# VectorE's own landing signal for K tiles, and a later place for w1, in a two-layer decode kernel

## The chip, the cores and the metric

The kernel runs on one core of one Trainium2 chip. A core has five engines with instruction queues of their own: PE (TensorE, matrix products), DVE (VectorE), ACT (ScalarE), POOL (GpSimd) and SP (SyncE, which here only issues transfers). They tell each other of finished work by semaphores. Sixteen DMA engines move data between the chip's memory (HBM) and the core's on-chip memory (SBUF, 128 partitions). The metric is the device time of one execution in microseconds (us), as the median of several runs.

## What is computed

Two identical rounds (called layers) of attention over a cache and a small mixer MLP, for one new token and a batch of two:

```python
x = A_x                                              # [2, 1, 576]
for _ in range(2):
    x = x + A(layernorm(x))
    x = x + B(layernorm(x))

def A(x):                                            # 32 heads of 128, 16384 cached positions
    q = (x @ wq).reshape(B, 1, 32, 128).transpose(0, 2, 1, 3)
    scores = einsum("bhqd,bhkd->bhqk", q, k_cache) * 128 ** -0.5
    o = einsum("bhqk,bhkd->bhqd", softmax(scores), v_cache)
    return o.transpose(0, 2, 1, 3).reshape(B, 1, 4096) @ wo

def B(x):
    h = gelu(layernorm(x) @ w1)
    hs = shifted(h) @ w2                             # shifts along a sequence of length 1
    x1 = x + hs
    return x1 + gelu(layernorm(x1) @ w3) @ w4
```

All inputs are bf16. K and V hold 2 x 32 x 16384 x 128 values each, 268 MB, and both layers read both of them. The shifts move every value of `h` out of a sequence of length one, so `hs` is the product of zeros with w2; the kernel computes `h` nevertheless, for both layers at once, at its very end.

## The kernel before

**Units and steps.** A unit is one head of one batch row; there are U = 64. Its K is one tile and its V another: 128 partitions x 32,768 bytes, 4.19 MB. A step of `attention` (L773 on) works on the K tile of one unit and the V tile of the unit before. Layer 0 takes the units in order; layer 1 starts with the last three (62, 63, 61), of which tiles are still on chip, and goes on with 0 to 60.

**What a step does.** The K tile has 128 blocks of 128 positions. PE and VectorE share them: for half of the blocks PE transposes eight at a time (`transposes`, L895), ScalarE copies them out of PSUM (`evacuate`, L906) and PE multiplies them with q (`scores`, L917); for the other half VectorE multiplies by a broadcast q and sums (`dots`, L943 and L947), four pairs of instructions in a step. The loop over `c` (0 to 7) writes the order of all engines down: scores run two chunks behind the transposes, so the last two chunks of a step are scored in the next step, at c = 0 and c = 1. VectorE's first pair of a step is at c = 0, the others at c = 2, 4 and 6; after the second pair come the maxima of the step before (`softmax_max`, L954 to L958), GpSimd's reduction over partitions (L960), and, on ScalarE, the exponentials (`softmax_exp`). PE's product with V (`pv`, L1001) is in four parts at c = 4 to 7. At c = 6 VectorE prepares the next unit's q (`q_broadcast`, L857 and L860), PE spreads it over the partitions (L864), and ScalarE copies it to `qb` (L867).

**Hardware loops and signals.** The steps 2 to 61 of layer 0 and 4 to 63 of layer 1 are "turning": three steps make one turn of a loop on PE, ACT and DVE, 120 steps in all. Inside a loop an engine can only wait on semaphores that belong to it alone (`_turn`: "a wait that no loop can hold"). The landing of a transfer has a semaphore without an owner. So GpSimd, which is not looped, waits for each landing and passes it on: `relay` (an increment, emitted at L201), called by `landed` at the start of a step for K and before `pv` for V. The relay's semaphore belongs to PE. VectorE learns of a landed K tile from PE: the score chunk that PE runs at c = 0 (after its first transposes of the new tile) writes the name `"go"`, and VectorE's first multiply of the step reads it.

**Slots and the plan.** On-chip memory for streamed data has six slots of the size of a tile (T bytes each). `plan_all` writes down, in order, every transfer of the kernel and its place. `Store.pump` issues the entries of this list strictly in order: if the head of the list needs cells that are still owned, everything behind it waits. A tile is released when its last reader is emitted; for a K tile in a turning step that is the last score of the step (c = 7). All transfers go through SP's queue (L100), which waits there for the readers of the old contents. In layer 1 the slots go round as (3, 0, 2, 5, 4, 1), so the end of the list of tiles is: (k,59) to slot 4, (v,58) to 1, (k,60) to 3, (v,59) to 0, (v,60) in two halves to 2. Then follow the weights: wo in three row pieces (slots 4, 4, 5), w3 in five pieces (slots 5, 5, 1, 1, 1), w4 in six (slots 1, 3, 3, 3, 3, 3). w1 of layer 1 (three DMAs of 576, 63 and 9 KB) lies in slot 4 behind wo's second piece; it is read by `h_projection` (L1049) after the output has been sent off. Its entry stands before the last two tiles, (v,59) and (v,60):

```python
        for i, (t, u) in enumerate(tiles):
            if i == len(tiles) - 2:
                self.plan_small("w1", 1, self.w1, 4 * T + 22 * row, (0, 56, 64))
            plan = self.plan_halves if i in (2, 4, len(tiles) - 1) else self.plan_tile
            plan(self.K if t == "k" else self.V, t, u, place[i])
```

**After the loop.** The last step (s = U) finishes the last unit; then `normalize`, wo, layer norms, w3 (L652, L657), gelu, w4 (L723), the transposes of the result and the transfer out follow, each bound to the one before.

Of the kernel before, what the change touches and what calls it, by code (L numbers as in the profile page):

```python
# [16 lines left out]
class Op:  # L17
# [4 lines left out]
    def __init__(self, eng, fn, sig=None, col=None):  # L22
        self.eng, self.fn, self.sig, self.col = eng, fn, sig, col
        self.deps, self.waits = [], []
        self.needed = self.relay = False
        self.val = self.sem = self.know = self.own = None

    @property
    def stream(self):
        return self.sem if self.sem is not None else "relay" if self.relay else self.eng  # L30


class Graph:
# [44 lines left out]
    def op(self, eng, fn, reads=(), writes=(), sig=None, col=None):  # L78
        return self._add(Op(eng, fn, sig, col), reads, writes)

    def relay(self, reads, writes):

        o = Op("gpsimd", None)
        o.relay = True
        return self._add(o, reads, writes)

    def dma(self, sem, starts, reads=(), writes=()):
# [45 lines left out]
    def emit(self):  # L133
        nc = self.nc
        self._waits()
        inside = {e: set() for e in self.LOOPED}
        for e in self.LOOPED:
            for first, (n, turns) in self.loops[e].items():
                inside[e].update(range(first, first + n * turns))
        users = {}  # L140
        for o in self.all:
            for d in o.waits:
                d.needed = True
                if o.eng in self.LOOPED and o.pos in inside[o.eng] and d.sem is None:
                    users.setdefault(id(d), set()).add(o.eng)
        for e in self.LOOPED:
            ops = self.ops[e]
            for first, (n, turns) in self.loops[e].items():
                for i in range(first, first + n):
                    same = ops[i:i + n * turns:n]  # L150
                    assert all(o.sig is not None and o.sig == same[0].sig for o in same), [o.sig for o in same]
                    some = any(o.needed for o in same)
                    who = set().union(*(users.get(id(o), ()) for o in same))
                    for o in same:
                        o.needed = some
                        if who:
                            users[id(o)] = who
                    if same[0].col is not None:
                        step = same[1].col - same[0].col
                        assert all(o.col == same[0].col + t * step for t, o in enumerate(same)), [o.col for o in same]  # L160
        done = {e: nc.alloc_semaphore(f"done_{e}") for e in self.ENGS if e != "sync"}
        own = {}
        count = {}
        for e in self.ENGS:
            for o in self.ops[e]:
                if o.sem is not None:
                    continue
                who = users.get(id(o), set())
                assert len(who) <= 1, (e, o.sig, who)
                o.own = "tensor" if o.relay else next(iter(who), None)  # L170
                o.needed = o.needed or o.relay
                if o.needed:
                    k = (o.stream, o.own)
                    count[k] = count.get(k, 0) + 1
                    o.val = count[k]
                    if o.own and k not in own:
                        own[k] = nc.alloc_semaphore(f"{o.stream}_{o.own}")
        for o in self.all:
            for d in o.waits:
                assert d.own in (None, o.eng), (o.eng, o.sig, d.eng, d.sig)  # L180

        def handle(k):
            s, who = k
            return self.dma_sems[s] if s in self.dma_sems else own[k] if who else done[s]

        def wait(eng, need, seen):
            for k, v in need.items():
                if v > 0 and seen.get(k, 0) < v:
                    eng.wait_ge(handle(k), v)
                    seen[k] = v  # L190

        def needs(o):
            need = {}
            for d in o.waits:
                k = (d.stream, d.own)
                need[k] = max(need.get(k, 0), d.val)
            return need

        def emit_op(eng, o, col=None):
            if o.relay:  # L200
                eng.sem_inc(own["relay", o.own], 1)  # L201
                return
            ins = o.fn(eng) if o.col is None else o.fn(eng, o.col if col is None else col)
            if o.sem is None and o.needed:
                ins.then_inc(handle((o.stream, o.own)), 1)

        def runner(e):
            def run(eng):
                seen, taken = {}, {}
                ops = self.ops[e]  # L210
                i = 0
                while i < len(ops):
                    if i in self.loops.get(e, ()):
                        n, turns = self.loops[e][i]
                        taken = self._turn(eng, ops, i, n, turns, taken, wait, needs, emit_op, handle)
                        seen = {k: v for k, v in seen.items() if not k[1]}
                        i += n * turns
                        continue
                    o = ops[i]
                    wait(eng, {k: v - taken.get(k, 0) for k, v in needs(o).items()}, seen)  # L220
                    emit_op(eng, o)
                    i += 1
            return run

        with nc.Block() as block:
            for e, sect in (("sync", block.sync), ("scalar", block.scalar), ("tensor", block.tensor),
                            ("vector", block.vector), ("gpsimd", block.gpsimd)):
                if self.ops[e]:
                    sect(runner(e))
# [93 lines left out]
class KB:  # L323
# [131 lines left out]
    def plan_all(self):  # L455

        T, U, n = self.TILE, self.U, self.KT - 1
# [4 lines left out]
        tiles = self.tile_order(0)  # L462
# [18 lines left out]
        tiles = self.tile_order(1)  # L481
        place = [0, 3] + [(3, 0, 2, 5, 4, 1)[i % 6] for i in range(2, len(tiles))]
        for i, (t, u) in enumerate(tiles):
            if i == len(tiles) - 2:
                self.plan_small("w1", 1, self.w1, 4 * T + 22 * row, (0, 56, 64))
            plan = self.plan_halves if i in (2, 4, len(tiles) - 1) else self.plan_tile
            plan(self.K if t == "k" else self.V, t, u, place[i])
        self.cuts["wo", 1] = [(0, 11, 4 * T), (11, 22, 4 * T + 11 * row), (22, 32, 5 * T)]
# [2 lines left out]
        self.cuts["w4", 1] = [(0, 8, w4_at)] + \  # L491
                             [(a, b, 3 * T + (a - 8) * row) for a, b in ((8, 16), (16, 24), (24, 30), (30, 34), (34, 36))]
        self.plan_rows("wo", 1, self.wo, self.cuts["wo", 1])
        self.plan_cols("w3", 1, self.w3, [at, at + w3r, T, T + w3r, T + 2 * w3r])
        self.plan_rows("w4", 1, self.w4, self.cuts["w4", 1])

# [265 lines left out]
    def attention(self, l):  # L762
# [4 lines left out]
        pend = []  # L767
# [9 lines left out]
        for s in range(U + 1):  # L777
# [5 lines left out]
            if l and s == U:  # L783
                self.home()
            if s < U and not self.kept(l, s):
                self.landed(l, "k", o[s])
            prompt, after = self.prompt(l, s), self.prompt(l, s - 1)
            n = self.pb(l, s) // self.CH
            for c in range(2 * n):
# [6 lines left out]
                    pend.append((s, u, c, self.chunk))  # L796
                    self.chunk += 1
                while pend and (len(pend) > LEAD or s == U):
                    self.scores(*pend.pop(0), go=turning and c == 0, of=(l, o[s]) if end else None)
                if s < U:  # L800
                    if c == 0 and prompt and s >= 1:
                        self.q_broadcast(o[s + 1], s + 1)
                    if c % n in (0, 2):
                        self.dots(l, s, u, h, c % n // 2, go=turning and c == 0)
                    if c == 2 * n - 2 and not prompt and s + 1 < max(U, leave + 1):
                        self.q_broadcast(o[s + 1] if s + 1 < U else u + 1, s + 1)
                if after:
# [35 lines left out]
        for t, k in ((self.o_acc, "o_acc"), (self.l, "l")):  # L843
            self.dv(lambda e, t=t: e.tensor_copy(out=t[:, at:at + 1], in_=t[:, 0:1]), reads=[k], writes=[k])

    def landed(self, l, t, u, last=False):

        if (t, u) in self.store.where:
            names = [(t, u)]
        else:  # L850
            names = [(t, u, h) for h in range(2)]
        for some in ([[nm] for nm in names] if last else [names]):
            self.g.relay([k for nm in some for k in self.store.keys(nm)], [("landed", nm) for nm in some])

    def q_broadcast(self, u, s):
        i = s % self.NS
# [50 lines left out]
                                        in_=self.tps[t][:, :].rearrange("p (i c) -> p i c", i=self.CH), func=ACT.Copy),  # L907
                 reads=[("tps", t)], writes=[("kt", k)], sig=("evac", c, t, k))

    def scores(self, s, u, c, at, go=False, of=None):  # L910

        k = at % self.NKT
        sp = s % self.NS
# [1 line left out]
        def f(pe):  # L915
# [1 line left out]
                ins = pe.matmul(self.sps[sp][:, c * self.CH + j:c * self.CH + j + 1], lhsT=self.kt[k][:, j, :],  # L917
                                rhs=self.q_col[:, sp:sp + 1], start=True, stop=True, skip_group_check=True)
            return ins
        reads, writes = [("q_col", sp), ("kt", k)], [("sps", sp)]  # L920
        if go:
            writes = writes + ["go"]
        last = []
        if of:
            for h in range(2):
                nm, _, keys = self.tile(of[0], "k", of[1], h * self.BP, self.BP)
                reads = reads + keys
                last.append(nm)
        self.pe(f, reads=reads, writes=writes, sig=("s", c, k, sp, go, of is not None))
        for nm in last:  # L930
            self.used(of[0], nm, self.CH)

    def dots(self, l, s, u, h, i, go=False):
        pb = self.pb(l, s)
        DB = (self.BP - pb) // 2
        r = s % self.NS
# [5 lines left out]
        c0 = (2 * h + i) * DB  # L942
        self.dv(lambda e: e.tensor_tensor(out=prod, in0=buf.rearrange("p (j d) -> p j d", d=128),  # L943
                                          in1=qbc, op=ALU.mult),
                reads=[("qb", r)] + keys + (["go"] if go else []), writes=["prod"], sig=("mult", r, c0, keys[0]))
        self.used(l, nm, DB)
        self.dv(lambda e: e.tensor_reduce(out=sd[:, c0:c0 + DB], in_=prod, axis=AX.X, op=ALU.add),  # L947
                reads=["prod"], writes=[("s_dve", r)], sig=("sum", r, c0))
# [159 lines left out]
```

## Time and profile before

| | |
|---|---|
| runs | 2597.4, 2594.4, 2595.95 us; median 2595.95 |
| profiled execution | 2597.14 us; span of its trace 2595.4 us |
| PE busy | 1598.9 us (62%) |
| VectorE busy | 1916.8 us (74%) |
| ScalarE busy | 1205.5 us (46%) |
| GpSimd busy | 51.5 us (2%) |
| SP's queue of transfers | 58798 packets, 1096.33 MB, 98.9% of 16 engines' span |
| VectorE L943 waiting for PE L917 | 529.9 us in 120 waits |
| chain that ended last | DVE 61%, PE 21%, issue 13%, DMA 3% |

How to read it. The page gives the busy time of each engine, and the span cut into 40 equal slices: a digit is the busy share of the slice in tenths, and the DMA row has the gigabytes per second under it. An answer by windows gives the same for any stretch: its bounds and length, the busy time and the number of instructions for PE, PEld (weight loads), DVE, ACT and POOL, the granted TensorE clock, the DMA share, GB/s. A row of the timeline is start, duration, engine, line and operation, result and operands; in brackets the idle time of the engine before it and who ended it. A row of waits is who waited, for whom, us in total, how often, and the longest. A row of issues ends with the median us from the issue of a transfer to its landing. "L943" is a line of the kernel.

### The profile page before, as it was taken

To read this page: it belongs to the slowest core of one execution; us is meant where nothing else is said; L and a number is where in the kernel's file an instruction comes from. 1 tells how busy PE (TensorE), PEld (TensorE's weight loads), DVE (VectorE), ACT (ScalarE), POOL (GpSimd) and SP (SyncE) were. 2 spreads that over 40 slices of the span, in tenths; PEclk is the share of its full clock that TensorE was granted. 3 is DMA by queue.
4 is the path that set the end of the run, shared out by engine and by line. 5 is a ranking of instruction groups with operands and counts; after the bars stand their busy time and mean duration, and the time that the engine had idled before them with its cause. 6 is when DMAs were issued, how large, how long until landed. Compare 5 with 4: busy or idle time off the path is not lost.

```text
span 2595.4 us, 74490 instructions
## 1 busy us (share of the span) xinstructions
PE 1598.9 (62%) x34309; PEld 1568.2 (60%) x34309; DVE 1916.8 (74%) x2048; ACT 1205.5 (46%) x1816; POOL 51.5 (2%) x149
## 2 busy tenths in 40 slices
PE   3656656656656656656666666666666666666665
PEld 3656656656656656656666665665665665665664
DVE  4777777777777777777568777777777777777773
ACT  3444544544544544544345444444444444444441
POOL 0000000000000000000000000000000000000000
PEclk8555655655555555555566555555555555555555
DMA  9999999999999999999999999999999999999959
GB/s 405 428 432 431 432 431 431 432 432 432 432 431 432 431 432 431 432 432 432 396 422 418 426 429 433 430 432 430 433 431 429 434 429 433 429 432 431 433 242 363
DMA packets 58851, 1097.09 MB, mean 423 GB/s; under 512 B 4778, under 2 KB 23342, under 8 KB 23854
## 3 DMA queue, kind: packets, MB, share of 16 engines
q1 hardware_dynamic: 58798, 1096.33, 98.9%
q8 instruction: 40, 0.66, 0.1%
q14 instruction: 13, 0.11, 0.0%
HBM read 1096.30 MB, written 0.00 MB: 422 GB/s over the span
## 4 chain that ended last, share of the span: by engine, by line
DVE 61%; PE 21%; issue 13%; DMA 3%; SPq 1%; DVEq 0%; ACT 0%; POOL 0%; POOLq 0%
DVE s_dve L947 33%; DVE prod L943 23%; PE tps L895 9%; PE mps L1001 8%; PE sps L917 2%; SPq L100 1%; PE sps L864 1%; DMA mem<-in_A_k_cache_dram 1%; DMA mem<-in_B_w_dram 1%; DVE diag L860 1%; DVE l L982 1%; DVE mx L956 1%; DVE q_col L857 1%; DVE mx L954 1%; DMA mem<-in_A_wo_dram 1%
## 5 line engine op out<-in xcount | busy, mean ns | idle before, releaser
L906 ACT ACTIVATE kt<-tps 128x1024 bf16<-128x1024 bf16 x1026 | 1037.2, 1024 | 710.1 <-PE tps L895 693.8
L947 DVE TENSOR_REDUCE s_dve<-prod 128x16 f32<-128x2048 bf16 x512 | 1168.3, 2282 | 17.6
L943 DVE TENSOR_TENSOR prod<-mem,qb 128x2048 bf16<-128x2048 bf16 x512 | 625.6, 1222 | 548.6 <-PE sps L917 529.9
L895 PE MATMUL tps<-ident,mem 128*128 128x128 bf16 x8208 | 998.2, 299 | 21.5 <-issue 13.1
L1001 PE MATMUL mps<-p,mem 128*128 128x1 bf16 x16384 | 515.0, 166 | 657.8 <-ACT p L973 639.0
L1001 PEld LDWEIGHTS mps<-p,mem 128*128 128x128 bf16 x16384 | 486.9, 104 | 669.0 <-ACT p L973 649.8
L895 PEld LDWEIGHTS tps<-ident,mem 128*128 128x128 bf16 x8208 | 762.0, 136 | 25.2 <-issue 16.6
L917 PEld LDWEIGHTS sps<-q_col,kt 128*128 128x128 bf16 x8208 | 411.3, 113 | 4.8 <-ACT kt L906 4.6
L917 PE MATMUL sps<-q_col,kt 128*128 128x1 bf16 x8208 | 400.3, 170 | 3.2 <-ACT kt L906 2.5
L968 ACT ACTIVATE mx<-mx 128x1 f32<-128x1 f32 x128 | 26.0, 203 | 386.0 <-POOL mx L960 386.0
L864 PE MATMUL sps<-diag,ones_bf 128*128 128x128 bf16 x129 | 37.1, 288 | 255.9 <-DVE diag L860 255.9
L864 PEld LDWEIGHTS sps<-diag,ones_bf 128*128 128x128 bf16 x129 | 13.5, 104 | 266.6 <-DVE diag L860 266.6
L867 ACT ACTIVATE qb<-sps 128x128 bf16<-128x128 f32 x129 | 35.8, 277 | 199.7 <-PE sps L864 199.7
L960 POOL PARTITION_ALL_REDUCE mx<-mx x128 | 49.3, 385 | 2487.8 <-DVE mx L958 2411.8
L970 ACT ACTIVATE p<-s_dve,mx 128x64 bf16<-128x64 f32 x128 | 44.5, 348 | 4.2
L973 ACT ACTIVATE p<-sps,mx 128x64 bf16<-128x64 f32 x128 | 37.6, 294 | 0.0
L956 DVE TENSOR_REDUCE mx<-sps 128x1 f32<-128x64 f32 x128 | 27.6, 215 | 11.7 <-PE sps L917 11.7
L723 PE MATMUL mps<-prod,mem 128*128 128x2 bf16 x680 | 20.7, 165 | 23.5 <-DMA mem<-in_B_w_dram 14.1
L723 PEld LDWEIGHTS mps<-prod,mem 128*128 128x128 bf16 x680 | 19.4, 104 | 25.0 <-DMA mem<-in_B_w_dram 12.2
L616 ACT ACTIVATE rstd<-rstd,eps 128x2 f32<-128x2 f32 x8 | 2.4, 295 | 65.8 <-DVE rstd L614 65.8
L860 DVE TENSOR_SCALAR diag<-ident,q_f 128x128 bf16<-128x128 bf16 x129 | 31.6, 245 | 0.3 <-PE sps L864 0.3
L703 DVE TENSOR_TENSOR x<-x,mps 128x8 f32<-128x8 f32 x4 | 0.7, 164 | 38.6 <-PE mps L723 38.6
(90 smaller groups left out, 245.3 us busy)
## 6 DMA issues: line engine op xcount, KB each, us to landing
mem<-in_A_v_cache_dram SPq DMA_DIRECT2D x124, 4096.0 KB, 32.1
mem<-in_A_k_cache_dram SPq DMA_DIRECT2D x122, 4096.0 KB, 31.3
mem<-in_B_w_dram SPq DMA_DIRECT2D x13, 1152.0 KB, 12.5
mem<-in_A_k_cache_dram SPq DMA_DIRECT2D x7, 2048.0 KB, 15.3
mem<-in_A_wq_dram SPq DMA_DIRECT2D x8, 1024.0 KB, 9.1
mem<-in_A_v_cache_dram SPq DMA_DIRECT2D x4, 2048.0 KB, 16.8
mem<-in_A_wo_dram SPq DMA_DIRECT2D x4, 1584.0 KB, 24.5
mem<-in_B_w_dram SPq DMA_DIRECT2D x6, 576.0 KB, 10.7
```

The costliest lines, as they stand in the source:

```text
L723: ins = pe.matmul(self.mps[:, t * B:(t + 1) * B], lhsT=buf[:, o:o + 128], rhs=rhs(k), start=(k == 0 and t == 0), stop=(k == last), skip_gr ...
L860: self.dv(lambda e, c: e.tensor_scalar(out=self.diag[:, :], in0=self.ident[:, :], scalar1=self.q_f[:, bass.ds(c, 1)], scalar2=None, op0=AL ...
L864: self.pe(lambda pe: pe.matmul(qps, lhsT=self.ones_bf[:, :], rhs=self.diag[:, :], start=True, stop=True, skip_group_check=True), reads=["o ...
L895: ins = pe.transpose(self.tps[t][:, j * 128:(j + 1) * 128], buf[:, j * 128:(j + 1) * 128], self.ident[:, :])
L906: self.act(lambda e: e.activation(out=self.kt[k][:, :, :], in_=self.tps[t][:, :].rearrange("p (i c) -> p i c", i=self.CH), func=ACT.Copy), ...
L917: ins = pe.matmul(self.sps[sp][:, c * self.CH + j:c * self.CH + j + 1], lhsT=self.kt[k][:, j, :], rhs=self.q_col[:, sp:sp + 1], start=True ...
L943: self.dv(lambda e: e.tensor_tensor(out=prod, in0=buf.rearrange("p (j d) -> p j d", d=128), in1=qbc, op=ALU.mult), reads=[("qb", r)] + key ...
L947: self.dv(lambda e: e.tensor_reduce(out=sd[:, c0:c0 + DB], in_=prod, axis=AX.X, op=ALU.add), reads=["prod"], writes=[("s_dve", r)], sig=(" ...
L956: self.dv(lambda e: e.tensor_reduce(out=mx[1], in_=self.sps[i][:, 0:n], axis=AX.X, op=ALU.max), reads=[("sps", i)], writes=[("mx1", i)], s ...
L960: self.pool(lambda e: e.partition_all_reduce(mx[3], mx[2], channels=128, reduce_op=ROP.max), reads=[("mx2", i)], writes=[("mx3", i)])
L970: self.act(lambda e: e.activation(out=p[:, n:self.NB], in_=self.s_dve[i][:, 0:self.NB - n], func=ACT.Exp, bias=mx[4], scale=self.scale, ac ...
L1001: ins = pe.matmul(self.mps[:, 448:449], lhsT=buf[:, j * 128:(j + 1) * 128], rhs=p[:, col:col + 1], start=(h == 0 and b == 0), stop=(h == 1 ...
```

## The change

GpSimd's `relay` now takes the engine that is to be told, and each such engine has a semaphore of its own (`landed_tensor`, `landed_vector`). In the turning steps `landed` sends two relays for a K tile, to PE and to VectorE, one after the other. VectorE's multiplies read the new name `("seen", tile)` where the first of them read `"go"`; the score chunk at c = 0 no longer writes `"go"`. In the plan of layer 1, w1's entry moves from before the last two tiles to between wo and w3; its place in memory stays. What is computed stays the same.

```diff
-    def relay(self, reads, writes):
+    def relay(self, to, reads, writes):
         o = Op("gpsimd", None)
-        o.relay = True
+        o.relay = f"landed_{to}"
+        o.own = to
         return self._add(o, reads, writes)
...
             if o.relay:
-                eng.sem_inc(own["relay", o.own], 1)
+                eng.sem_inc(own[o.stream, o.own], 1)
                 return
...
         for i, (t, u) in enumerate(tiles):
-            if i == len(tiles) - 2:
-                self.plan_small("w1", 1, self.w1, 4 * T + 22 * row, (0, 56, 64))
             plan = self.plan_halves if i in (2, 4, len(tiles) - 1) else self.plan_tile
...
         self.plan_rows("wo", 1, self.wo, self.cuts["wo", 1])
+        self.plan_small("w1", 1, self.w1, 4 * T + 22 * row, (0, 56, 64))
         self.plan_cols("w3", 1, self.w3, [at, at + w3r, T, T + w3r, T + 2 * w3r])
...
             if s < U and not self.kept(l, s):
-                self.landed(l, "k", o[s])
+                self.landed(l, "k", o[s], both=turning)
...
-                    self.scores(*pend.pop(0), go=turning and c == 0, of=(l, o[s]) if end else None)
+                    self.scores(*pend.pop(0), of=(l, o[s]) if end else None)
...
-                        self.dots(l, s, u, h, c % n // 2, go=turning and c == 0)
+                        self.dots(l, s, u, h, c % n // 2, told=turning)
...
         for some in ([[nm] for nm in names] if last else [names]):
-            self.g.relay([k for nm in some for k in self.store.keys(nm)], [("landed", nm) for nm in some])
+            keys = [k for nm in some for k in self.store.keys(nm)]
+            self.g.relay("tensor", keys, [("landed", nm) for nm in some])
+            if both:
+                self.g.relay("vector", keys, [("seen", nm) for nm in some])
...
-        reads, writes = [("q_col", sp), ("kt", k)], [("sps", sp)]
-        if go:
-            writes = writes + ["go"]
+        reads = [("q_col", sp), ("kt", k)]
...
-                reads=[("qb", r)] + keys + (["go"] if go else []), writes=["prod"], sig=("mult", r, c0, keys[0]))
+                reads=[("qb", r)] + keys + ([("seen", nm)] if told else []), writes=["prod"], sig=("mult", r, c0, keys[0]))
```

The rest of the diff renames what the two parts need.

## The prediction

> **What bounds the kernel now.** I read the page's slices and queue shares first, then the queue's own waits, then time-ordered rows around the odd slice, then the steady step.
>
> ```profile
> span 2595.4 us, 74490 instructions
> DMA  9999999999999999999999999999999999999959
> GB/s 405 428 432 431 432 431 431 432 432 432 432 431 432 431 432 431 432 432 432 396 422 418 426 429 433 430 432 430 433 431 429 434 429 433 429 432 431 433 242 363
> ```
>
> The page: the DMA engines are full from start to end, at 432 GB/s in a steady slice. A K or V tile is 128 x 32,768 B = 4.194 MB, so two of them (one step of the loop) take 8.389 / 0.432 = 19.42 us. One slice, the last but one, falls to 242 GB/s: of its 64.9 us, (432 - 242) / 432, some 28 us, are empty. The empty stretch, window by window (us, busy time of PE, PEld, DVE, ACT, POOL, clock, DMA share, GB/s):
>
> ```profile
> 2495.00:2500.00 5.00, 0.90 (x33) 0.90 (x34) 4.93 (x8) 0.94 (x5) 0.35 (x1) 0.60 0.99 426
> 2500.00:2505.00 5.00, 3.10 (x69) 3.02 (x66) 4.93 (x5) 2.05 (x2) 0.00 (x0) 0.50 0.00 0
> ...
> 2520.00:2525.00 5.00, 2.96 (x76) 2.88 (x74) 4.35 (x5) 2.24 (x3) 0.00 (x0) 0.50 0.00 0
> 2525.00:2530.00 5.00, 5.00 (x108) 5.00 (x106) 1.27 (x2) 2.63 (x4) 0.00 (x0) 0.50 0.42 125
> ```
>
> SP's longest wait from 2490 us on, and its issues in order of time:
>
> ```profile
> SPq L100 <- PE sps L917: 38.7, 1, 38.7
> ```
>
> ```profile
> 2487.64 0.33 SPq L100 DMA_DIRECT2D mem<-in_A_k_cache_dram  x1
> 2526.70 1.25 SPq L100 DMA_DIRECT2D mem<-in_B_w_dram  x3
> 2527.99 1.29 SPq L100 DMA_DIRECT2D mem<-in_A_v_cache_dram  x3
> 2529.33 24.84 SPq L100 DMA_DIRECT2D mem<-in_A_wo_dram  x3
> ```
>
> SP issued the last K tile, (k,60), at 2487.64 and then stood 38.7 us for a score of PE, because the next entry of the plan is w1. By the placement rule w1 lies in slot 4, which (k,59) holds until the last score of step 62. Behind it stood (v,59), whose slot 0 had been free since (v,56) was consumed in step 60, and (v,60), whose slot 2 came free a step before slot 4.
>
> Why is slot 4 so late? Landing times of K, in windows 100-200, 1100-1200, 1400-1500 and 2300-2400 us (last number: median us from issue to landing):
>
> ```profile
> mem<-in_A_k_cache_dram SPq DMA_DIRECT2D x5, 4096.0 KB, 33.4
> mem<-in_A_k_cache_dram SPq DMA_DIRECT2D x4, 4096.0 KB, 31.4
> mem<-in_A_k_cache_dram SPq DMA_DIRECT2D x5, 4096.0 KB, 15.0
> mem<-in_A_k_cache_dram SPq DMA_DIRECT2D x5, 4096.0 KB, 13.8
> ```
>
> They shrink slowly: compute is a hair slower than the transfers (19.33 us twice, 19.73 once in three issues, mean 19.46, against 19.42). In layer 1 a K tile lands some 14 us after issue and is used two steps, 39 us, after it: compute runs 25 us behind. (k,60) landed at 2487.64 + 13.9 = 2501.5 and its first multiply began at 2528.69. So the lag is compute's, and one step shows whose:
>
> ```profile
> 2465.79 0.25 DVE L860 TENSOR_SCALAR diag<-ident,q_f 128x128 bf16<-128x128 bf16 x1
> 2466.09 0.29 PE L864 MATMUL sps<-diag,ones_bf 128*128 128x128 bf16 x1 [2.04 <-DVE diag L860]
> ...
> 2466.42 0.28 ACT L867 ACTIVATE qb<-sps 128x128 bf16<-128x128 f32 x1 [1.50 <-PE sps L864]
> ...
> 2469.80 0.40 PE L917 MATMUL sps<-q_col,kt 128*128 128x1 bf16 x8
> ...
> 2470.30 1.23 DVE L943 TENSOR_TENSOR prod<-mem,qb 128x2048 bf16<-128x2048 bf16 x1 [4.27 <-PE sps L917]
> ```
>
> VectorE ends its step at 2466.04 and stands 4.27 us for the "go" score of PE, although its operands (the K tile, and qb at 2466.70) are there. Over the run that is 529.9 us in 120 waits, one for each loop step.
>
> **The semaphore edit.** It removes 120 waits on "go"; it adds 120 increments on GpSimd and, in the go's place, 120 waits of VectorE. Behind that wait stands everything VectorE does in a step (four multiplies and sums, the maxima, keep, diag), and GpSimd's all-reduce, ScalarE's exponentials and PE's PV matmuls wait for those. With the tile landed, the new wait ends at once and the multiply goes to qb: 2466.70 + 0.05 instead of 2470.30, 3.55 us earlier. The step's floor is then 19.33 - 3.55 = 15.78 us. Can PE keep that? Its first PV of a step comes 9.1 us after VectorE's first multiply (2450.97 to 2460.05); counted from 2466.75 that is 2475.8, and PE was through its transposes and scores at 2473.6. The maxima come 7.1 us after the multiply, at 2473.8, and the scores they need ended at 2471.3. Yes.
>
> The increment has no row of its own. The relay to PE at 2541.87 was followed by PE's matmul at 2542.01, so at most 0.14 us for both. GpSimd's sequencer holds the all-reduce behind it; GpSimd is busy 51.5 us of the run. Bounds over 120 steps: 0, and 120 x 0.14 = 17 us if nothing covered it. I take 0: the cover is 19.42 - 15.78 = 3.6 us of slack per step.
>
> But 3.55 us x 120 = 426 us isn't to be had: transfers at 19.42 take over as soon as the lag is eaten. In layer 1 25 us go at 3.6 us a step in seven steps; with 60 loop steps, 25 / 60 = 0.42 us a step would be enough. In the steady part the transfers were never idle, so the gain there is nothing. It is worth something where they starved at the entry of layer 1's loop:
>
> ```profile
> 1396.00:1400.00 4.00, 4.00 (x99) 4.00 (x100) 0.00 (x0) 1.42 (x3) 0.00 (x0) 0.50 0.83 291
> 1400.00:1404.00 4.00, 4.00 (x66) 4.00 (x62) 3.79 (x3) 3.87 (x4) 0.00 (x0) 0.54 0.90 385
> ```
>
> (432 - 291) / 432 x 4 + (432 - 385) / 432 x 4 = 1.7 us, bounds 0 and 3 (smaller dips near it). And it releases slot 4 about 20 us earlier, which the second edit needs.
>
> The DMA: Bandwidth & Descriptors page of the Trainium skill (Specifications) speaks against all this: it gives a core 358 GB/s from HBM. By that, two tiles would take an estimated 23.4 us, steps would be bound by transfers already, and the first edit would be worth nothing: about 2567. The slices say 432, and the trace decides.
>
> **w1 behind wo.** Moved: one wait and three DMAs of 576, 63 and 9 KB, issued in 1.25 us, on SP's queue past (v,59), the two halves of (v,60) and the three wo pieces. No other queue issues it. Its only reader is the projection at the very end (L1049, 2592.69). Before, (v,59) landed at 2527.99 + 13.9 = 2541.9. After, (k,60) is followed at once: 2501.5 + 9.71 = 2511.2, 30.7 us earlier. w1's 0.664 MB come back between wo and w3: 1.5 us at 432 GB/s, 1.8 at the 374 of the wo windows. Net 29.0 (28.8 to 29.2); the empty windows alone, 25 + 0.58 x 5 = 27.9, are the lower bound.
>
> The same page's fit (Anatomy of one DMA) puts a fixed 2.0 us on a transfer; by it the hole would be 2526.7 - 2501.5 + 2.0 = 27.2 and the sum about 2567. The landing rows contain this restart already.
>
> What is late next? Each slot must be free before the queue runs dry. wo takes slot 4 by 2521 ((v,60)'s new landing): with compute at the transfers' heels, step 62 ends near 2500. w4 needs slot 3, (k,60)'s, near 2547: step 63 ends near 2519. The chain behind (v,60), counted by the rows of before (7.6 us from first PV to last score, 1.9 to the last step's PV, 3.6 for it, 1.9 to wo), would have two wo pieces done at 2531, two before the third lands at 2533.3. Then w3, w4 and the last 4.5 us behind w4's landing keep their distances; they were bound by landings before, too.
>
> **Sum.** 29.0 + 1.7 = 30.7. The profiled execution took 2597.14 us, 1.7 outside its 2595.4 span; it would take 2566.4. The three runs' median is 2595.95, so **2565.3**.
>
> **Rivals.**
> 1. VectorE's wait only changes its name (qb, a maximum, or GpSimd's queue still ties it to PE): step stays 19.46 and only w1's move counts. Then transfers go dry at 2521 until slot 4 is freed at 2526.7; all weights land by 2570, and compute sets the end: step 63 starts at 2528.7 as before, its PV no longer waits for (v,59) (4.2 us), wo runs in 4.9, w4 in 5.7 without waiting for landings: 2582. For it: the chain of waits is full of VectorE and PE. Against: qb was ready 3.6 us early. 6%.
> 2. Compute catches up only partly (0.15 us a step, 9 of 25 us): half-way, 2573. 3%.
> 3. Slower: with the queue filled deeper and VectorE reading a tile as it lands, the transfer rate falls. It decides above 30.7 / 2557 = 1.2%; at 1.5% the price is 38 us: 2604. Against: layer 0, with 33 us of queue, and layer 1, with 14, both show 432. 3%.
> 4. The edits do nothing, or the gain is given back to another stop before w1's place: 2596. 2%.
>
> **Numbers.** The forecast gets 86%. The range, 2562 (every starved spot gone) to 2573 (rival 2's end, or several us lost behind (v,60)), leaves out about 2 in 10. About 0.2%, 5 us, is what a measurement can tell from no change. Faster 0.95, same 0.02, slower 0.03.
>
> **What would show it.** No empty DMA slice near the end; (v,59) issued within 1 us of (k,60) and (v,60) before (k,60)'s landing; no wait of VectorE on L917 before L943, but waits on the landing, mean near 3.6 us, and K's landing time in layer 1 rising from 15 towards 40 us; step 19.42. Wrong if the DMA share shows a hole at wo, if steps stay 19.46 with K landing at 14 us, or if the steady slices fall under 430 GB/s.

## The result, and the profile after

The changed kernel takes 2564.07 us (median of four runs, 2563.42 to 2564.72) against 2596.68 for the kernel before: a ratio of 0.9876, 95% interval 0.9859 to 0.9893. The forecast was 2565.3, the range 2562 to 2573. The kernel before scatters more than the others, from 2594.40 to 2600.23 us over all its runs, so a gain against it is good to a few us only; differences of 1 or 2 us below are between kernels that carry the change, or a part of it.

First the page's head: the span, the busy tenths of the DMA engines and their GB/s in 40 slices.

```profile
span 2561.9 us, 74650 instructions
...
DMA  9999999999999999999999999999999999999999
GB/s 409 426 432 433 432 432 431 433 432 431 431 433 431 431 431 433 431 431 431 417 410 428 432 431 431 433 431 431 431 433 432 431 431 433 431 431 431 434 431 360
```

The slice that had 242 GB/s is gone; the last one, 360, holds the small-row weights and the 4.4 us between their last landing and the end of the span. The chain that ended last, by engine, has turned round: where VectorE had 61% of it, the transfers now have 64%.

```profile
DMA 64%; DVE 24%; issue 6%; PE 5%; SPq 1%; ACT 0%; POOLq 0%; DVEq 0%; POOL 0%
```

SP's issues in order of time (start, duration, transfer):

```profile
2456.52 0.33 SPq L101 DMA_DIRECT2D mem<-in_A_k_cache_dram  x1
2457.38 19.40 SPq L101 DMA_DIRECT2D mem<-in_A_v_cache_dram  x3
2495.38 23.50 SPq L101 DMA_DIRECT2D mem<-in_A_wo_dram  x3
2518.93 31.36 SPq L101 DMA_DIRECT2D mem<-in_B_w_dram  x14
2559.81 0.28 SPq L101 DMA_DIRECT2D out_dram<-prod  x1
```

(v,59) follows (k,60) after 0.86 us; the three V issues are through at 2476.8. wo, which needs slot 4, goes out at 2495.38, where slot 4 came free at 2526.7 before. K's landing times, in windows 1100-1200, 1400-1500 and 2300-2400 us (the last number), and VectorE's wait:

```profile
mem<-in_A_k_cache_dram SPq DMA_DIRECT2D x4, 4096.0 KB, 40.7
mem<-in_A_k_cache_dram SPq DMA_DIRECT2D x6, 4096.0 KB, 28.8
mem<-in_A_k_cache_dram SPq DMA_DIRECT2D x6, 4096.0 KB, 40.7
```

```profile
DVE prod L944 <- POOLq L202: 483.4, 112, 4.5
```

A K tile is now issued 40.7 us before it lands, and used at once: compute waits for transfers, not the other way round. VectorE still stands idle nearly as long as before (529.9 us then), but at the landing, which GpSimd passes on (POOLq L202), and not at a score of PE. One step of layer 1, in order of time:

```profile
2415.15 0.25 DVE L863 TENSOR_SCALAR diag<-ident,q_f 128x128 bf16<-128x128 bf16 x1
2415.45 0.29 PE L867 MATMUL sps<-diag,ones_bf 128*128 128x128 bf16 x1 [1.51 <-DVE diag L863]
...
2415.78 0.28 ACT L870 ACTIVATE qb<-sps 128x128 bf16<-128x128 f32 x1 [0.97 <-PE sps L867]
...
2419.64 1.03 PE L898 MATMUL tps<-ident,mem 128*128 128x128 bf16 x8 [1.15 <-POOLq L202]
2419.77 1.23 DVE L944 TENSOR_TENSOR prod<-mem,qb 128x2048 bf16<-128x2048 bf16 x1 [4.37 <-POOLq L202]
```

PE and VectorE start the new tile 0.13 us apart, both on GpSimd's word; before, VectorE began 1.3 us behind PE's first transposes (2470.30 against 2468.99 in the step that the prediction shows). The next view shows the lag being eaten, by SP's issues early in layer 1:

```profile
1409.11 0.33 SPq L101 DMA_DIRECT2D mem<-in_A_k_cache_dram  x1
...
1424.86 0.33 SPq L101 DMA_DIRECT2D mem<-in_A_k_cache_dram  x1
...
1440.61 0.33 SPq L101 DMA_DIRECT2D mem<-in_A_k_cache_dram  x1
...
1487.85 0.33 SPq L101 DMA_DIRECT2D mem<-in_A_k_cache_dram  x1
...
1504.59 0.33 SPq L101 DMA_DIRECT2D mem<-in_A_k_cache_dram  x1
```

As long as tiles lie ready, a step takes 15.75 us; from 1487.85 on it lengthens, and late in the layer it is 19.4 (2437.10 to 2456.52), the time of two tiles.

### The profile page after: what moved, and what is told of

It reads as the page before. It is cut to its first block, busy times and chain, and to the rows that moved or that the text cites. A ratio compares the mean times of both kernels' runs of the same rounds, so it can differ in the third digit from the quotient of the medians.

```text
span 2561.9 us, 74650 instructions
## 1 busy us (share of the span) xinstructions
PE 1610.7 (63%) x34309; PEld 1577.1 (62%) x34309; DVE 1916.6 (75%) x2048; ACT 1204.5 (47%) x1816; POOL 51.5 (2%) x149
## 4 chain that ended last, share of the span: by engine, by line
DMA 64%; DVE 24%; issue 6%; PE 5%; SPq 1%; ACT 0%; POOLq 0%; DVEq 0%; POOL 0%
DMA mem<-in_A_k_cache_dram 61%; DVE s_dve L948 13%; DVE prod L944 9%; PE mps L1002 2%; PE tps L898 2%; DMA mem<-in_B_w_dram 1%; SPq L101 1%; DMA mem<-in_A_v_cache_dram 1%; DMA mem<-in_A_wo_dram 1%; PE sps L867 1%; DMA mem<-in_A_wq_dram 0%; PE sps L920 0%; PE mps L723 0%; DVE diag L863 0%; DVE l L983 0%
## 5 line engine op out<-in xcount | busy, mean ns | idle before, releaser
L944 DVE TENSOR_TENSOR prod<-mem,qb 128x2048 bf16<-128x2048 bf16 x512 | 625.5, 1222 | 515.9 <-POOLq L202 483.4
L723 PEld LDWEIGHTS mps<-prod,mem 128*128 128x128 bf16 x680 | 19.4, 104 | 23.7 <-DMA mem<-in_B_w_dram 12.6
L981 DVE COPY o_acc<-mps 128x1 f32 (+1 forms) x128 | 20.2, 158 | 12.0 <-PE mps L1002 12.0
## 6 DMA issues: line engine op xcount, KB each, us to landing
mem<-in_A_k_cache_dram SPq DMA_DIRECT2D x122, 4096.0 KB, 40.7
```

The lines of the kernel that those rows point to most:

```text
L723: ins = pe.matmul(self.mps[:, t * B:(t + 1) * B], lhsT=buf[:, o:o + 128], rhs=rhs(k), start=(k == 0 and t == 0), stop=(k == last), skip_gr ...
```

## The experiments

**w1's move alone.** The kernel before, with only w1's entry moved.

```diff
-            if i == len(tiles) - 2:
-                self.plan_small("w1", 1, self.w1, 4 * T + 22 * row, (0, 56, 64))
...
         self.plan_rows("wo", 1, self.wo, self.cuts["wo", 1])
+        self.plan_small("w1", 1, self.w1, 4 * T + 22 * row, (0, 56, 64))
```

> Only w1's entry is moved; VectorE still waits for the score of PE. My theory (the lag of compute is what holds slot 4): a step stays at 19.46 us, compute is still 25 us behind at the end, the transfers run dry for some 7 us ahead of wo, and compute sets the end: 2582 us (2578 to 2586). Rival (w1's place in the plan alone makes the hole): 2567 us, no empty slice.

Measured: 2583.63 us (2582.45 to 2583.85), ratio 0.9947, interval 0.993 to 0.9964. VectorE's wait and three windows of this kernel (us, busy PE, PEld, DVE, ACT, POOL, clock, DMA share, GB/s):

```profile
DVE prod L942 <- PE sps L916: 531.2, 120, 8.1
```

```profile
2520.00:2525.00 5.00, 2.96 (x76) 2.88 (x75) 4.32 (x5) 2.27 (x3) 0.00 (x0) 0.50 0.01 3
2525.00:2530.00 5.00, 5.00 (x108) 5.00 (x106) 1.30 (x2) 2.63 (x4) 0.00 (x0) 0.50 0.41 116
...
2575.00:2580.00 5.00, 4.34 (x142) 4.02 (x139) 0.94 (x4) 0.00 (x0) 0.00 (x0) 0.50 0.01 3
```

The V tiles go out early, then the transfers run dry ahead of wo, as slot 4 is still late; and at the very end they are done (the last weights land at 2570.4) while PE still works, until 2582.0: compute, some 25 us behind at the last K tiles, sets the end. w1's move alone is worth 12.9 us.

**The semaphore alone.** The changed kernel with w1's entry back before the last two tiles (the same diff, reversed).

> Only the semaphore; w1's entry stays ahead of the last two tiles. My theory, as the trace of the changed kernel sharpens it: slot 4 comes free near 2495.4 us and the last K tile lands near 2497.3, so the queue stands at w1 but the engines hardly run dry: a hole of 0 to 3 us, 2564 to 2568 us. Rival (the place of w1 is worth the 29 us that the prediction put beside it): 2592 to 2596 us, the hole stays.

Measured: 2566.67 us (2566.33 to 2566.71), ratio 0.9883, interval 0.9867 to 0.99. SP's issues and the windows around them:

```profile
2456.60 0.33 SPq L101 DMA_DIRECT2D mem<-in_A_k_cache_dram  x1
2495.46 1.26 SPq L101 DMA_DIRECT2D mem<-in_B_w_dram  x3
2496.76 1.29 SPq L101 DMA_DIRECT2D mem<-in_A_v_cache_dram  x3
```

```profile
2490.00:2495.00 5.00, 3.50 (x83) 3.41 (x80) 3.15 (x4) 1.99 (x3) 0.00 (x0) 0.50 0.79 341
2495.00:2500.00 5.00, 3.87 (x80) 3.79 (x78) 2.42 (x2) 2.49 (x3) 0.00 (x0) 0.50 0.81 264
```

SP still stands 38.9 us at w1, from 2456.60 to 2495.46, as long as before. But it now stands there while 40 us of transfers are queued. The engines only thin out: (432 - 341) / 432 x 5 + (432 - 264) / 432 x 5 = 3.0 us, which is about what is missing: 2.6 us against the whole change. The semaphore alone is worth 29.8 us.

**VectorE's floor, by doubled work.** The changed kernel, with extra work behind the first sum of each loop step: one more sum, one more multiply and sum, or two more sums. The results are the same values written again. The lines are shortened, and the two comments, which the kernels don't have, tell the three apart.

```diff
+        if told and h == 0 and i == 0:
+            for _ in range(1):                       # 2 in the third kernel
+                self.dv(lambda e: e.tensor_tensor(out=prod, ...     # second kernel alone
+                self.dv(lambda e: e.tensor_reduce(out=sd[:, c0:c0 + DB], in_=prod, axis=AX.X, op=ALU.add),
+                        reads=["prod"], writes=[("s_dve", r)], sig=("sum", r, c0))
```

> The changed kernel with the first sum of each of the 120 loop steps done twice (2.29 us of VectorE each). My theory: the floor of a step goes from 15.8 to 18.1 us, still under the 19.43 of two tiles: 2564 us (2563 to 2567), VectorE's wait for the landing falls by 2.3 us a step. Rival (VectorE is on the path, as its 75% busy share and its share of the chain suggest): 120 x 2.29 = 275 us more, 2839 us.

> The changed kernel with the first multiply and sum of each loop step done twice (3.58 us from multiply to multiply). My theory: floor 15.78 + 3.58 = 19.36 us against 19.43: the lag is hardly eaten, w1's move alone works: 2578 us (2570 to 2583), K landing some 15 to 20 us after issue in layer 1. Rival 1 (the floor does not matter as long as it is below the transfers): 2564 us. Rival 2 (VectorE on the path): 2985 us.

> The changed kernel with the first sum of each loop step done three times (2 x 2.29 us more). My theory: floor 15.78 + 4.58 = 20.36 us, over the 19.43 of two tiles: now compute sets the step. Against the kernel with w1 moved alone (2583.6 us, step 19.46) the 120 loop steps cost 120 x (20.36 - 19.46) = 108 us: 2691 us (2680 to 2702), steps 20.3 to 20.4 us, starved transfers in the steady slices (under 425 GB/s). Rival (VectorE's work stays hidden whatever its size): 2564 us.

| extra in a step | floor worked out | measured us | against before, interval |
|---|---|---|---|
| none | 15.78 | 2564.07 | 0.9859 to 0.9893 |
| one sum | 18.07 | 2564.68 | 0.9859 to 0.9892 |
| multiply and sum | 19.36 | 2574.84 | 0.9897 to 0.993 |
| two sums | 20.36 | 2693.75 | 1.0336 to 1.0396 |

With one more sum, 275 us of VectorE's work are put in, and the medians differ by 0.6, with overlapping runs. VectorE's wait with one more sum, and K's landing in windows 1400-1500 and 2300-2400 with one more multiply and sum:

```profile
DVE prod L944 <- POOLq L202: 200.1, 98, 2.1
```

```profile
mem<-in_A_k_cache_dram SPq DMA_DIRECT2D x5, 4096.0 KB, 14.3
...
mem<-in_A_k_cache_dram SPq DMA_DIRECT2D x5, 4096.0 KB, 18.9
```

The wait shrinks by about what was put in (483.4 to 200.1, 283 us). At a floor of 19.36 layer 1 eats only 4.6 us of its lag in some 46 steps, 0.1 us a step, and the end is 10.8 us later than with the change alone. Two more sums pass the transfers: most slices of that kernel show 403 to 419 GB/s, and SP's K issues are 20.4 us apart:

```profile
715.94 0.33 SPq L101 DMA_DIRECT2D mem<-in_A_k_cache_dram  x1
...
736.33 0.33 SPq L101 DMA_DIRECT2D mem<-in_A_k_cache_dram  x1
...
756.75 0.33 SPq L101 DMA_DIRECT2D mem<-in_A_k_cache_dram  x1
```

So what counts is whether the floor lies below or above the 19.43 us of two tiles, and how much of the lag it eats; the runs show it on both sides.

**Which layer.** The semaphore in one loop only, in the other one "go" as before; w1 moved in both.

```diff
-                self.landed(l, "k", o[s], both=turning)
+                self.landed(l, "k", o[s], both=turning and l == 1)        # or 0
...
-                    self.scores(*pend.pop(0), of=(l, o[s]) if end else None)
+                    self.scores(*pend.pop(0), go=turning and c == 0 and l != 1, of=(l, o[s]) if end else None)
...
-                        self.dots(l, s, u, h, c % n // 2, told=turning)
+                        self.dots(l, s, u, h, c % n // 2, told=turning and l == 1, go=turning and c == 0 and l != 1)
```

> VectorE told by GpSimd in layer 1's loop only; in layer 0's by PE's score, as before; w1 moved. My theory: all that the end needs is layer 1's; the 3 us that the landings gained between the layers came from layer 0's earlier end, and are lost: 2567 us (2566 to 2568). Rival (the gain between the layers comes from the entry of layer 1's loop, as the prediction had it): 2564 us.

> VectorE told by GpSimd in layer 0's loop only; in layer 1's by PE's score; w1 moved. My theory: layer 1 keeps its lag, so the end is that of w1's move alone, less the 3 us between the layers: 2579 us (2575 to 2583). Rival (what is gained in layer 0 is carried to the end): 2567 us.

Measured: layer 1 only 2565.75 us (2564.47 to 2566.42; 0.9859 to 0.9892), layer 0 only 2582.32 us (2580.04 to 2582.88; 0.9923 to 0.9957), and the changed kernel, run again beside them, 2563.85 (2563.60 to 2564.06).

> The changed kernel itself, beside the kernels of this call on the same chip: 2564 us (2563 to 2566).

The end belongs to layer 1: without its semaphore the time is that of w1's move alone, less some 1.3 us, with overlapping runs that did not stand side by side. Near the end (window 2300-2400 us) a K tile lands 14.1 us after its issue with layer 0 only and 40.7 with layer 1 only: the lag of compute is back, or gone. Layer 0's semaphore is worth 1.9 us, between what the theory (3) and its rival (0) expected: neither had it right. VectorE's waits in the kernel with layer 1 only show both kinds beside each other:

```profile
DVE prod L944 <- PE sps L920: 267.5, 60, 8.0
...
DVE prod L944 <- POOLq L202: 229.1, 53, 4.4
```

**w1 behind everything.** The changed kernel, with w1's entry at the end of the plan.

```diff
-        self.plan_small("w1", 1, self.w1, 4 * T + 22 * row, (0, 56, 64))
         self.plan_cols("w3", 1, self.w3, [at, at + w3r, T, T + w3r, T + 2 * w3r])
         self.plan_rows("w4", 1, self.w4, self.cuts["w4", 1])
+        self.plan_small("w1", 1, self.w1, 4 * T + 22 * row, (0, 56, 64))
```

> w1's entry behind w4's, the last of the plan. My theory: transfers set the end, so taking w1's 0.66 MB out of the way of w3 and w4 brings the last w4 piece, and the end, 1.5 us forward: 2562.5 us; w1 lands before its reader comes. Rival (w1's few small DMAs cost nothing where they stand, or its reader then waits for it): 2564 to 2566 us.

Measured: 2562.19 us (2561.86 to 2562.80), 1.66 below the changed kernel run beside it, with no overlap of the runs; against before 0.9862, interval 0.9846 to 0.9879. The last product of w4 and w1's reader:

```profile
2555.31 1.16 PE L723 MATMUL mps<-prod,mem 128*128 128x2 bf16 x30 [0.72 <-DMA mem<-in_B_w_dram]
...
2557.74 0.83 PEld L1050 LDWEIGHTS sps<-xn,mem 128*128 128x128 bf16 x25 [0.22 <-DMA mem<-in_B_w_dram]
2557.75 0.92 PE L1050 MATMUL sps<-xn,mem 128*128 128x4 bf16 x25
```

The last piece of w4 lands 1.5 us earlier (2556.0 instead of 2557.5). PE shows no idle time ahead of w1's reader, and its weight load the same 0.22 us as in the kernel before: w1's 1.5 us of transfer now lie under the last sums and the transposes of the result. But it is w1's landing that ends these 0.22 us, so there is nothing left to spare. This is the fastest version of this study.

## Why the prediction was right, and where it was not

**What bounds.** Right: transfers at 432 GB/s were full except for one hole and smaller dips between the layers, and compute lagged. The doubled work shows both halves of it.

**The step's floor.** Predicted 15.78, seen 15.75 while the lag was eaten in layer 1. The step afterwards, predicted 19.42, is 19.4. VectorE's wait for the landing was put near 3.6 us and is 483.4 / 112 = 4.3: the 3.6 left out that the idle time runs from the end of diag (VectorE's last instruction of a step), 0.7 us before qb, and not from qb. The time isn't touched by this.

**The hole.** Predicted 29.0. (k,60) landed 4.3 us earlier in the profile after, and the end of the span came 33.5 earlier: 29.2 fall behind (k,60). The figure held, for both edits together.

**Where its gain was put.** This is the step that failed: "w1 behind wo ... Net 29.0", with 1.7 for the semaphore, as if the 29.0 were w1's. The parts measured alone are 29.8 us for the semaphore, 12.9 for w1's move, 32.6 together. The prediction saw that the semaphore frees slot 4 "about 20 us earlier, which the second edit needs", and didn't draw the other half of it (nor the size: slot 4 came free 31.3 us earlier): with slot 4 free at 2495.4 and the last K tile landing at 2497.3, w1 in its old place has hardly anything to hold up. The hole was a product of two things, w1's place and a late slot, and either one away shrinks it. With w1 moved alone, the late slot and compute's lag set the end, as the first rival had it: worked out as 2582, measured as 2583.63, in the kernel that it describes. The total was right because the prediction reckoned the 29.0 with slot 4 already early; it had no price for the semaphore without w1's move.

**The starved spots.** Predicted 1.7 at the entry of layer 1's loop and nothing from layer 0. The sum of the forecast, 30.7, came to 32.6 between the medians. The kernel with the semaphore in layer 1 only is 1.9 us above the whole change, so about that much comes from layer 0, which the prediction put at nothing. The profiles of these two show where: the last V tile of layer 0 lands at 1263.3 us in both, but w3's second piece, which waits for its place, is issued at 1272.6 instead of 1274.3, and the first K tile of layer 1 lands at 1318.8 instead of 1320.6. So the end of layer 0, no longer behind the transfers, frees the places of the weights sooner. What the entry of layer 1's loop gives beside this stays open. Of the 4.3 us by which (k,60) landed earlier, 2.9 are there at layer 1's first K tile (0.8 of them at the kernel's first), so 1.4 would be left; but the last K tile lands 1.1 us later in the kernel with w1 last than in the changed one, though nothing differs ahead of it. That the sum fell short by just 1.9 proves nothing, as the kernel before scatters by more.

**The increment and GpSimd's queue.** Taken as 0. One of the last K tiles landed at 2477.83; GpSimd's two increments stand at 2477.85 and 2477.93, PE starts at 2477.92 and VectorE at 2478.05. VectorE is served second, its increment 0.08 us later than PE's. With 3.6 us of slack in a step this costs nothing. (The 2541.87 that the prediction gives as the relay's time is the landing; the increment stands at 2541.90, so its bound of 0.14 holds.)

**The 358 GB/s.** The Trainium skill's 358 GB/s for a core (DMA: Bandwidth & Descriptors, Specifications) is no bound of this run: steady slices show 431 to 434 GB/s after the change, with VectorE waiting for the landing in 112 of 120 loop steps. The specification's row divides the bandwidth of a stack between two cores, and every run here is of one. The 2.0 us that the prediction takes from the same page (Anatomy of one DMA) is there a fit to transfers which GpSimd issues, while SP issues these; by it the hole was 27.2, and 29.2 were measured.

**The other rivals.** A rate that falls with a deeper queue didn't show: 40.7 us of queue and 431 to 433 GB/s, as with 14 us. The half-way case is met by the kernel with the doubled multiply and sum: 2574.84 us, with most of the lag left.

## What to carry to other kernels

A hole in the transfers has a place (who stands at the head of the queue) and a cause (why the buffer is late); price each alone and both together, since the parts needn't add up: here 29.8 and 12.9 make 33. A lag of compute behind transfers costs nothing while the stream lasts and is paid at its end (some 25 us of lag cost 19.6 here, w1's move alone against the whole change). A floor clearly below the transfers' step eats it (15.78 and 18.07 us against 19.43), however little the engine's idle time falls. What is read last should be loaded last.

## What was not expected of the hardware

VectorE's idle time says little about its worth: 529.9 us before, 483.4 after a gain of 33 us, 200.1 in a kernel that takes the same time within its scatter. An issue of many small rows can hold SP for long, though it waits for no semaphore. In the kernel with w1 last the second piece of wo, 1,408 rows of 1,152 bytes, held SP for 18.6 us, until 2.4 us before the last tile ahead of it landed, and the engines stayed full all the while (412 to 439 GB/s). In the kernel with w1's move alone, where the tiles had landed before, the same issue took 0.74 us.
